# Attention into FFN on one core: transposes of four head pairs moved from TensorE to DMA, with the early slots rebuilt around them

## The chip, the cores and the metric

One core of one Trainium2 chip. The metric is device time in microseconds (us); lower is better. Verdicts compare fast runs of one kernel with fast runs of the kernel before, made on the same chip in the same rounds. PE is TensorE, DVE is VectorE, ACT is ScalarE, POOL is GpSimd, SP is SyncE. A DMA "lands" when all its data have arrived. An idle is "released" by the instruction or DMA whose end let the engine go on.

## The reference, cut to what matters

```python
# q, k, v: (8, 8, 576, 64) float32.  Sd = 144 (sequence pooled by 4)
out_d     = softmax(scale * mean4(q) @ mean4(k).T) @ mean4(v)      # pooled attention
out_local = softmax(where(|i - j| < 4, scale * q @ k.T, -1e9)) @ v # narrow band
x   = (repeat(out_d, 4) + out_local) as 4608 tokens x 512
out = (relu(x @ w_gate) * (x @ w_val)) @ w_out                     # d_ff = 1536
```

## The kernel before

Heads are handled two at a time, in 32 "pairs". Four pairs of heads make one batch entry, that is 576 tokens. The first four pairs are a fill phase. Then the program runs in "slots": slot s works on the attention of pair s + 4, and beside it on three of the twelve column tiles of the FFN of token chunk s // 4 (512 tokens). From slot 4 on each slot also computes one output tile y of the chunk before. PE, DVE, ACT, POOL and SP each execute their own instructions strictly in the order in which the code emits them.

q and k have to be transposed before the scores. Pairs 0 to 8 do it on PE, by 24 small matmuls into PSUM and copies back; these also give the pooled q and k. Pairs 9 on do it by one DMA transpose issued from SP, and DVE sums by four afterwards (`emit_pool`).

```python
NTP = 9                                   # pairs below this are transposed on PE

def emit_load(hp):                        # on the GpSimd queue, fp32 to fp16 (but for the first q)
    ...
    elif hp < NTP:                        # one DMA for q, one for k
    else:                                 # one DMA per head: two for q, two for k
    ...
def emit_qkT(hp):
    nc.sync.dma_start_transpose(out=qkT[hp % 4][...], in_=qk16[hp % NL]...)

def emit_slot(s, gate):
    c, jj, hp = s // 4, 3 * (s % 4), s + LEAD
    ...
    emit_in(hp + 4)                       # loads, four pairs ahead
    if NTP <= hp + 3 < NP:
        emit_qkT(hp + 3)                  # DMA transpose, three pairs ahead
    if s == 0:
        ...                               # ends with emit_qkT_pe(hp + 1, 2, 3)
    if s <= 5:
        ...
        emit_s2t(hp - 1, gate)            # values of the pair before; then on ACT: Ln, gate, Exp; on DVE: xn, xT
    ...
    if s == 4:
        emit_y(c - 1, s % 4, 1)           # first y tile: 12 matmuls
    else:
        emit_h(c, jj, 0)()                # FFN column tile: 8 matmuls, relu on ACT, product on DVE
    emit_s1(hp, 4)                        # scores of this pair, exponentials
    if s == 4:
        emit_h(c, jj, 0)()
    emit_h(c, jj + 1, 1)()
    if s == 4:
        emit_vd(hp, 5)
    else:
        emit_qkT_pe(hp + 1, 4, 0, True)   # transposes of the next pair on PE
    return emit_h(c, jj + 2, 3)
```

The weights arrive in slices on the same GpSimd queue: a quarter of w_gate and w_val with each of pairs 3, 5, 6 and 7, and all of w_out, in four pieces, after pair 8.

The softmax here doesn't subtract the row's maximum and nothing guards it: scores larger than these inputs give would overflow.

Of the kernel before, what the change touches and what calls it, by code (L numbers as in the profile page):

```python
# [57 lines left out]
def kernel(  # L58
# [22 lines left out]
    NCH = NTOK // TCH  # L81
    NJJ = D_FF // 128
    LEAD = 4
    NTP = 9
    NVP = 9
    NK = NJJ // 2
    B0 = 1
# [88 lines left out]
    def emit_load(hp):  # L176
        r = hp % NL
        b, off = head_off(hp)
        for src, dst in ((q, qk16[r][:, 0, :]), (k, qk16[r][:, 1, :])):
            if hp == 0 and src is q:  # L180
                nc.sync.dma_start(
                    q32.rearrange("p (n d) -> p n d", d=64),
                    _dap(src, off, [[D, 96], [NQ * D, 2 * NB], [1, D]]),
                )
                nc.scalar.copy(out=dst, in_=q32)
            elif hp < NTP:
                nc.gpsimd.dma_start(
                    dst.rearrange("p (n d) -> p n d", d=64),
                    _dap(src, off, [[D, 96], [NQ * D, 2 * NB], [1, D]]),
                )  # L190
            else:
                dv = dst.rearrange("p (j h d) -> p j h d", h=2, d=64)
                for hh in range(2):
                    nc.gpsimd.dma_start(  # L194
                        dv[:, :, hh, :],
                        _dap(src, off + hh * S * D, [[D, 96], [NQ * D, NB], [1, D]]),
                    )
        base = off - 3 * D
        t = vw[r][:, :, 0:64]
        n = 2 * NB  # L200
        if off == 0:
            nc.gpsimd.dma_start(
                t[:, 1:, :], _dap(v, base + NQ * D, [[D, WK], [NQ * D, n - 1], [1, D]])
            )
            nc.gpsimd.dma_start(t[3:WK, 0, :], _dap(v, 0, [[D, WK - 3], [1, D]]))
            nc.gpsimd.dma_start(t[0:3, 0, :], _dap(v, 0, [[D, 3], [1, D]]))
        elif b == B - 1 and hp % NPB == NPB - 1:
            nc.gpsimd.dma_start(
                t[:, 0 : n - 1, :], _dap(v, base, [[D, WK], [NQ * D, n - 1], [1, D]])
            )  # L210
            last = base + (n - 1) * NQ * D
            nc.gpsimd.dma_start(t[0:99, n - 1, :], _dap(v, last, [[D, 99], [1, D]]))
            nc.gpsimd.dma_start(t[99:WK, n - 1, :], _dap(v, last, [[D, WK - 99], [1, D]]))
        else:
            nc.gpsimd.dma_start(t, _dap(v, base, [[D, WK], [NQ * D, n], [1, D]]))  # L215
        if hp >= NVP:
            nc.gpsimd.dma_start(
                v4[hp % NV4], _dap(v, off, [[4 * D, 72], [72 * 4 * D, 4], [1, 4 * D]])
            )
# [13 lines left out]
                op=ALU.add,  # L233
            )

    def emit_qkT_pe(hp, b0, b1, b0_last=False):
        r, r4, r2 = hp % NL, hp % 4, hp % 2
        sv = qk16[r].rearrange("p i (h j d) -> p i h j d", h=2, d=64)
        blocks = list(range(2 * NB))
        if hp == 0:  # L240
            blocks = blocks[NB:] + blocks[:NB]
        elif b0_last:
            blocks = blocks[4:] + blocks[:4]
        for n in blocks:
            lo = 120 * (n % 4)
            bank = b0 if n < 4 else b1 + n // 4 - 1
# [10 lines left out]
        act, dve = nc.scalar.copy, nc.vector.tensor_copy  # L257
        if hp == 0:
            plan = ((2, 1, act), (2, 0, act), (1, 1, dve), (1, 0, dve), (0, 1, act), (0, 0, dve))
        elif b0_last:  # L260
            plan = ((1, 1, act), (1, 0, act), (2, 1, dve), (2, 0, dve), (0, 1, dve), (0, 0, act))
        else:
            plan = ((0, 1, act), (0, 0, act), (1, 1, dve), (2, 1, dve), (2, 0, dve), (1, 0, act))
        for i, pooled, copy in plan:
# [30 lines left out]
            out=vd[hp % 3].rearrange("p c (x d) -> p c x d", x=3)[:, :, 0:3:2, :], in_=o[0:72]  # L295
        )

    def emit_s1(hp, p0):
        r4, r2 = hp % 4, hp % 2
        for c in range(2):  # L300
            for hh in range(2):
                lo = 64 * hh
                nc.tensor.matmul(  # L303
                    out=ps[0:72, p0 + 2 * c + hh, 288:432],
                    lhsT=qkd[r2][lo : lo + 64, 1, bass.ts(c, 72)],
                    rhs=qkd[r2][lo : lo + 64, 0, :],
                    start=True,
                    stop=True,
                )
            for j in range(3 * c, 3 * c + 3):  # L310
                for hh in range(2):
                    lo = 64 * hh
                    k0 = S + NQ * j - 3
                    nc.tensor.matmul(  # L314
                        out=ps[:, p0 + 2 * c + hh, NQ * (j % 3) : NQ * (j % 3) + NQ],
                        lhsT=qkT[r4][lo : lo + 64, k0 : k0 + 128],
                        rhs=qkT[r4][lo : lo + 64, NQ * j : NQ * j + NQ],
                        start=True,
                        stop=True,
                    )  # L320
        for g in range(2):
            o = ee[r2][:, :, 288 * g : 288 * g + 288]
            nc.scalar.activation(  # L323
                out=o, in_=ps[0:WK, p0 + 2 * g : p0 + 2 * g + 2, 0:288], func=AF.Exp, scale=scale
            )
            nc.vector.tensor_tensor(  # L326
                out=o,
# [1 line left out]
                in1=_sap(masks_sb, (0, WK), 288 * g, [[0, 2], [1, 288]]),  # L329
                op=ALU.mult,  # L330
            )
        nc.scalar.activation(  # L332
            out=ed[r2][:, :, 0 : 2 * SD].rearrange("p h (c t) -> p c h t", c=2),
            in_=ps[0:72, p0 : p0 + 4, 288:432].rearrange("p (c h) t -> p c h t", c=2),
            func=AF.Exp,
            scale=scale / 16.0,
        )

    def emit_s2(hp, bank, pu):
        r2 = hp % 2  # L340
# [38 lines left out]
                op=ALU.mult,  # L379
            )  # L380

    def emit_s2t(hp, between):
        r2 = hp % 2
        e, d = ee[r2], ed[r2]
        for g in range(2):
            for hh in range(2):
                nc.tensor.matmul(
                    out=ps[64 * hh : 64 * hh + 64, 4 + g, 0:288],
                    lhsT=ones_sb[0:WK, 0:64],
                    rhs=e[:, hh, 288 * g : 288 * g + 288],  # L390
                    start=True,
                    stop=True,
                )
            for c in range(2):
                for hh in range(2):
                    nc.tensor.matmul(  # L396
                        out=ps[64 * hh : 64 * hh + 64, 4 + g, 288:360],
                        lhsT=ones_sb[0:72, 64:128],
                        rhs=d[:, hh, c * SD + 72 * g : c * SD + 72 * g + 72],
                        start=(c == 0),  # L400
# [2 lines left out]
        for g in range(2):  # L403
            for j in range(3):
                for hh in range(2):
                    nc.tensor.matmul(
                        out=ps[64 * hh : 64 * hh + 64, 2 + g, NQ * j : NQ * j + NQ],
                        lhsT=vw[hp % NL][:, NB * hh + 3 * g + j, 0:64],
                        rhs=e[:, hh, 288 * g + NQ * j : 288 * g + NQ * j + NQ],
                        start=True,  # L410
# [2 lines left out]
            for c in range(2):  # L413
                for hh in range(2):
                    nc.tensor.matmul(
                        out=ps[64 * hh : 64 * hh + 64, 2 + g, 288:360],
                        lhsT=vd[hp % 3][:, c, 128 * hh : 128 * hh + 64],
                        rhs=d[:, hh, c * SD + 72 * g : c * SD + 72 * g + 72],
                        start=(c == 0),
                        stop=(c == 1),  # L420
                    )
        r, x = rden[r2], xn[r2]
        nc.scalar.activation(out=r, in_=ps[:, 4:6, 0:360], func=AF.Ln)  # L423
        between()
        nc.scalar.activation(out=r, in_=r, func=AF.Exp, scale=-1.0)  # L425
        nc.vector.tensor_tensor(out=x, in0=ps[:, 2:4, 0:360], in1=r, op=ALU.mult)  # L426
        emit_xsum(hp)

    def emit_xsum(hp):
# [216 lines left out]
    def emit_wo(i):  # L646
# [2 lines left out]
            _dap(moe_w_out, 384 * i * D_MODEL, [[D_MODEL, 128], [128 * D_MODEL, 3], [1, D_MODEL]]),  # L649
        )  # L650

    after_load = {3: 0, 5: 1, 6: 2, 7: 3}

    def emit_in(hp):
# [5 lines left out]
        if hp in after_load:  # L660
            emit_wslice(after_load[hp])
        if hp == 8:
            for i in range(4):
                emit_wo(i)

    def emit_warm(n):
# [52 lines left out]
    def emit_slot(s, gate):  # L719
        c, jj, hp = s // 4, 3 * (s % 4), s + LEAD  # L720
        if NVP <= hp + 1 < NP:
            emit_vd_pool(hp + 1)
        emit_in(hp + 4)
        if NTP <= hp + 3 < NP:
            emit_qkT(hp + 3)
        if s == 0:
# [2 lines left out]
            emit_h_mm(c, jj, 3, 0, range(1))  # L729
            emit_x_pe(hp - 1, 0)  # L730
            emit_h(c, jj, 3, ((0, range(1, 4)), (1, range(3, 4))))()
            emit_s1(hp, 2)
            emit_h(c, jj + 1, 0)()
            emit_vd(hp, 6)
            emit_qkT_pe(hp + 1, 2, 3)
            return emit_h(c, jj + 2, 3)
        if s <= 5:
            if s == 5:
                emit_pool(hp)
            elif s < 4:  # L740
                emit_vd(hp, 1)
            emit_s2t(hp - 1, gate)
        elif gate:
            gate()
        if s > 4:
            if hp < NP:
                emit_y(c - 1, s % 4, 1 if s == 5 else 2, 6 if s == 5 else 2, lambda: emit_s1(hp, 4))
            else:
                emit_y(c - 1, s % 4, 2)
            if hp < NVP:  # L750
                emit_vd(hp, 3)
            if hp + 1 < NP:
                emit_pool(hp + 1)
            emit_h(c, jj, 0)()
            if 24 <= s < 28:
                emit_wt(s - 24)
            if hp < NP:
                emit_s2w(hp)
            emit_h(c, jj + 1, 1)()
            gate = emit_h(c, jj + 2, 0)  # L760
            if hp < NP:
                gate()
                emit_xsum(hp)
                return None
            return gate
        if s == 4:
            emit_y(c - 1, s % 4, 1)
        else:
            emit_h(c, jj, 0)()
        emit_s1(hp, 4)  # L770
        if s == 4:
            emit_h(c, jj, 0)()
        emit_h(c, jj + 1, 1)()
        if s == 4:
            emit_vd(hp, 5)
        else:
            emit_qkT_pe(hp + 1, 4, 0, True)
        return emit_h(c, jj + 2, 3)

    with tc.manual_schedule(engines={ET.PE, ET.DVE, ET.Activation, ET.SP, ET.Pool}):  # L780
        nc.scalar.dma_start(cst_sb[:, 960:1080], cst_dr[:, 960:1080])
# [57 lines left out]
```

## Time and profile before

| | before |
|---|---|
| median of 3 runs | 354.75 us (354.53 to 354.94) |
| span of the profiled run | 352.6 us |
| PE busy | 343.5 us (97%) |
| start on PE of slots 1 to 5 | 32.92, 41.22, 49.51, 57.46, 67.18 us |
| last load of pairs 5 to 8 landed | 26.2, 33.0, 40.0, 46.8 us |

The page of the kernel before cuts the span into 40 slices. A digit is a busy share in tenths; PEclk is the granted clock of TensorE in tenths; the DMA row is the mean busy share of the 16 DMA engines.

```profile
PE   6999999999999999999999999999999999999996
PEclk9999999999999999999999999999999999999999
DMA  9999999999999999999999999940000000101013
```

PE is full from the second slice on, at full clock. The DMA engines are full too, up to the 26th slice. In the first 57 us the reason is a backlog: loads wait in the GpSimd queue behind one another, and the view of DMA issues gives this for the last load of pair 8 (the last number is us from issue to landing; it was issued at 36.1 us):

```profile
qk<-in_k_dram POOLq DMA_DIRECT2D x1, 144.0 KB, 10.7
```

So it took 10.7 us to land at 46.8 us. The next view has one row for each of the slots 1 to 4: the stretch, its length, then busy time of each engine with the number of instructions, the granted clock, the DMA share and GB/s.

```profile
32.92:41.22 8.30, 8.04 (x106) 4.52 (x104) 5.09 (x10) 6.11 (x12) 5.32 (x8) 1.00 1.74 186
41.22:49.51 8.29, 8.03 (x105) 4.52 (x103) 5.09 (x10) 6.10 (x12) 4.42 (x6) 1.00 1.69 188
49.51:57.46 7.95, 7.69 (x98) 4.09 (x96) 5.09 (x10) 6.11 (x12) 3.78 (x5) 1.00 1.69 184
57.46:67.18 9.72, 9.72 (x91) 4.95 (x90) 6.60 (x8) 5.66 (x10) 9.55 (x13) 1.00 1.87 166
```

Slots 1 and 2 take 8.3 us, with 0.26 us of PE idle. PE's own timeline (start, length, what) shows what an ordinary slot pays for the transposes, and how slot 4 is ordered:

```profile
46.59 0.82 PE L248 MATMUL ps<-cst_sb,qk 96*64 96x120 f16 x24
...
58.36 2.76 PE L530 MATMUL ps<-wo_sb,gT 128*128 128x512 f16 x12
...
61.56 1.04 PE L505 MATMUL ps<-xT,wg_sb 128*128 128x512 f16 x4
```

The 24 transposing matmuls (L248) hold PE for 0.75 us to the next start (47.34 us). In slot 4, which starts at 57.46 us, the y tile (L530) runs from 58.36 to 61.05 us. Meanwhile DVE computes the attention output of pair 7:

```profile
60.06 0.91 DVE L426 TENSOR_TENSOR xn<-ps,rden 128x720 f16<-128x720 f32 x1
61.00 0.76 DVE L431 TENSOR_TENSOR xT<-xn 128x576 f16<-128x576 f16 x1
```

xT (L431) ends at 61.76 us, 4.3 us after the start of the slot. The FFN matmuls of chunk 1, which need it, start at 61.56 us, and the one that needs pair 7 is their fourth. It comes in time: PE has no idle in this slot. In all of 24 to 90 us PE's waits come to 1.1 us; three of them are for xn (the fourth, of 0.3 us, is for ee in slot 5):

```profile
PE ps L505 <- DVE xn L426: 0.8, 3, 0.3
```

### The profile page before, as it was taken

The numbers are of one execution on the slowest core, as the hardware profiler recorded it, in microseconds if no ns is written. First come the engines' busy times: TensorE is split into PE (matmuls) and PEld (weight loads), VectorE is DVE, ScalarE is ACT, GpSimd is POOL, SyncE is SP. The second block draws the span as 40 slices with busy tenths as digits, with TensorE's granted clock in tenths as the row PEclk, the third lists the DMA queues.
The fourth block names the chain that finished last, engine by engine and source line by source line (L and its number), as shares of the span: only waits on it lengthen the run. The fifth ranks groups of instructions, "written<-read, shape, count | busy, mean of one in ns | idle before, by whom it ended". The sixth has DMA issues, their size and how long they took to land.

```text
span 352.6 us, 7540 instructions
## 1 busy us (share of the span) xinstructions
PE 343.5 (97%) x2947; PEld 187.0 (53%) x2947; DVE 248.3 (70%) x397; ACT 214.0 (61%) x370; POOL 189.5 (54%) x233
## 2 busy tenths in 40 slices
PE   6999999999999999999999999999999999999996
PEld 3665555545545555555555544455555465655575
DVE  5894666687786677788887787776777655354581
ACT  3867776676677766666666667667667533333332
POOL 8986557999999877777778877722100000000000
PEclk9999999999999999999999999999999999999999
DMA  9999999999999999999999999940000000101013
GB/s 153 168 171 187 182 194 153 180 167 194 176 146 166 171 131 131 134 134 118 134 119 138 113 131 140 123 95 30 32 31 32 33 30 30 46 30 46 15 47 119
DMA packets 168770, 40.26 MB, mean 114 GB/s; under 512 B 150080, under 2 KB 165664, under 8 KB 168736
## 3 DMA queue, kind: packets, MB, share of 16 engines
q0 software_dynamic: 132960, 22.93, 86.1%
q1 hardware_dynamic: 32176, 10.55, 17.6%
q10 hardware_dynamic: 3600, 6.32, 5.3%
q8 instruction: 23, 0.38, 0.5%
q14 instruction: 11, 0.09, 0.1%
HBM read 46.45 MB, written 9.44 MB: 159 GB/s over the span
## 4 chain that ended last, share of the span: by engine, by line
PE 89%; DVE 4%; ACT 4%; DMA 1%; issue 1%; POOLq 0%
PE ps L505 50%; PE ps L530 18%; PE ps L592 8%; PE ps L448 3%; PE ps L248 2%; PE ps L314 2%; PE ps L303 2%; PE ps L456 2%; DMA qk<-in_k_dram 1%; DVE xn L426 1%; ACT rden L423 1%; DVE xo L375 1%; ACT rden L425 1%; DVE ee L326 1%; ACT r L520 1%
## 5 line engine op out<-in xcount | busy, mean ns | idle before, releaser
L505 PE MATMUL ps<-xT,wg_sb 128*128 128x512 f16 x432 | 111.5, 379 | 0.9 <-DVE xn L426 0.8
L505 PE MATMUL ps<-xT,wv_sb 128*128 128x512 f16 x432 | 111.2, 379 | 0.5 <-DVE gT L521 0.5
L521 DVE TENSOR_TENSOR gT<-r,ps 128x512 f16<-128x512 f16 x108 | 71.8, 683 | 49.2 <-PE ps L505 32.4
L520 ACT ACTIVATE r<-ps 128x512 f16<-128x512 f32 x108 | 64.0, 593 | 38.2 <-PE ps L505 35.7
L530 PE MATMUL ps<-wo_sb,gT 128*128 128x512 f16 x288 | 70.1, 380 | 0.0
L505 PEld LDWEIGHTS <-wv_sb 128*128 128x128 f16 x432 | 42.1, 98 | 51.4 <-issue 0.8
L472 DVE TENSOR_TENSOR xn<-ps,rden 64x720 f16<-64x720 f32 x46 | 41.6, 905 | 39.2 <-ACT rden L469 38.5
L505 PEld LDWEIGHTS <-wg_sb 128*128 128x128 f16 x432 | 39.7, 97 | 39.5 <-issue 0.7
L323 ACT ACTIVATE ee<-ps 112x576 f16<-112x576 f32 x64 | 38.1, 647 | 26.2 <-PE ps L314 25.4
L466 ACT ACTIVATE rden<-ps 64x720 f32<-64x720 f32 x46 | 35.2, 764 | 12.9 <-PE ps L456 12.3
L530 PEld LDWEIGHTS <-gT 128*128 128x128 f16 x288 | 26.1, 98 | 30.0
L326 DVE TENSOR_TENSOR ee<-ee,cst_sb 112x576 f16<-112x576 f16 x64 | 40.8, 674 | 1.3 <-ACT ee L323 1.1
L275 POOL TENSOR_TENSOR vd<-v 72x256 f16<-72x256 f32 x23 | 17.7, 770 | 44.2 <-PE ps L456 43.5
L194 POOL DMA_DIRECT2D qk<-in_q_dram x46 | 34.1, 744 | 4.2 <-DMA wo_sb<-in_moe_w_out_dram 2.8
L194 POOL DMA_DIRECT2D qk<-in_k_dram x46 | 33.2, 728 | 0.6 <-DMA qk<-in_k_dram 0.4
L215 POOL DMA_DIRECT2D vw<-in_v_dram x30 | 28.4, 946 | 4.9 <-PE ps L396 1.4
L229 DVE TENSOR_REDUCE qkd<-qkT 128x288 f16<-128x1152 f16 x23 | 30.8, 1341 | 0.0
L274 POOL TENSOR_TENSOR v<-v 72x512 f32<-72x512 f16 x23 | 30.5, 1327 | 0.3
L538 ACT COPY y_sb<-ps 128x512 f32<-128x512 f32 x24 | 14.1, 587 | 17.2 <-PE ps L530 17.2
L431 DVE TENSOR_TENSOR xT<-xn 128x576 f16<-128x576 f16 x28 | 22.3, 798 | 0.2
L448 PE MATMUL ps<-ee,vw 112*128 112x96 f16 x276 | 20.4, 205 | 0.3 <-DVE ee L326 0.3
L332 ACT ACTIVATE ed<-ps 72x576 f16<-72x576 f32 x32 | 20.5, 642 | 0.0
(97 smaller groups left out, 374.4 us busy)
## 6 DMA issues: line engine op xcount, KB each, us to landing
out_dram<-y_sb ACTq DMA_DIRECT2D x24, 256.0 KB, 4.0
vw<-in_v_dram POOLq DMA_DIRECT2D x30, 168.0 KB, 6.3
qk<-in_q_dram POOLq DMA_DIRECT2D x46, 72.0 KB, 3.4
qk<-in_k_dram POOLq DMA_DIRECT2D x46, 72.0 KB, 3.6
v<-in_v_dram POOLq DMA_DIRECT2D x23, 144.0 KB, 6.2
out_dram<-y_sb SPq DMA_DIRECT2D x22, 128.0 KB, 1.7
wg_sb<-in_moe_w_gate_dram POOLq DMA_DIRECT2D x4, 384.0 KB, 9.8
wv_sb<-in_moe_w_val_dram POOLq DMA_DIRECT2D x4, 384.0 KB, 10.7
```

What stands on the lines that cost most here:

```text
L194: nc.gpsimd.dma_start(dv[:, :, hh, :], _dap(src, off + hh * S * D, [[D, 96], [NQ * D, NB], [1, D]]),)
L229: nc.vector.tensor_reduce(out=qkd[hp % 2].rearrange("p i t -> p (i t)"), in_=qkT[hp % 4][:, 0 : 2 * S].rearrange("p (t f) -> p t f", f=4), ...
L274: nc.gpsimd.tensor_tensor(out=m, in0=t[:, :, 0:128], in1=t[:, :, 128:256], op=ALU.add)
L323: nc.scalar.activation(out=o, in_=ps[0:WK, p0 + 2 * g : p0 + 2 * g + 2, 0:288], func=AF.Exp, scale=scale)
L326: nc.vector.tensor_tensor(out=o, in0=o, in1=_sap(masks_sb, (0, WK), 288 * g, [[0, 2], [1, 288]]), op=ALU.mult,)
L448: nc.tensor.matmul(out=ps[:, bank, NQ * j : NQ * j + NQ], lhsT=vflat[:, v0 : v0 + 128], rhs=e[:, hh, lo : lo + NQ], start=True, stop=True,)
L466: nc.scalar.activation(out=r[lo : lo + 64], in_=ps[de : de + 64, 4 + 2 * hh : 6 + 2 * hh, 0:360], func=AF.Ln)
L472: nc.vector.tensor_tensor(out=x[lo : lo + 64], in0=ps[lo : lo + 64, 4 + 2 * hh : 6 + 2 * hh, 0:360], in1=r[lo : lo + 64], op=ALU.mult,)
L505: nc.tensor.matmul(out=pair(pp)[:, which, :], lhsT=w[:, kk, bass.ts(jj, 128)], rhs=xT[:, kk, c * TCH : (c + 1) * TCH], start=(kk == 0), st ...
L520: nc.scalar.activation(out=r1, in_=h1, func=AF.Relu)
L521: nc.vector.tensor_tensor(out=gT[c % 2][:, jj, :], in0=r1, in1=h2, op=ALU.mult)
L530: nc.tensor.matmul(out=y_ps, lhsT=gT[c % 2][:, jj, bass.ts(ty, 128)], rhs=wo_sb[:, jj, :], start=(jj == 0), stop=(jj == NJJ - 1),)
```

## The change

The intent is to take the transposing matmuls of pairs 5 to 8 off PE. The pairs go by DMA transposes, with DVE's sum by four in place of the pooled copies. Their q and k are then loaded by one DMA per head, two per tensor. The slots are rewritten: PSUM bank pairs rotate from slot to slot, the pooled exponential of a pair comes first, the first y tile moves from the start to the end of slot 4, and half of w_out is loaded after the q and k of pair 9.

```diff
-    NTP = 9
+    NTP = 5
@@ emit_load: between the loads of q, k and those of v
+        if hp == 9:
+            emit_wo(2)
+            emit_wo(3)
@@ emit_in
         if hp == 8:
-            for i in range(4):
+            for i in range(2):
                 emit_wo(i)
@@ emit_s1(hp, p0, p1=None, ed_first=False): scores may lie in two bank pairs that are not neighbours
+        base = (p0, p0 + 2 if p1 is None else p1)
+        def pooled():
+            nc.scalar.activation(
+                out=ed[r2]...,
+                in_=_sap(ps, (0, 72), 512 * base[0] + 288,
+                         [[512 * (base[1] - base[0]), 2], [512, 2], [1, 144]]),
+                func=AF.Exp, scale=scale / 16.0)
@@ slots; EARLY[s] is (numerator, denominator, first FFN tile, scores, scores), as bank pairs
+    EARLY = {1: (1, 2, 0, 2, 3), 2: (2, 3, 1, 0, 3), 3: (3, 0, 2, 0, 1), 4: (0, 1, 3, 1, 2)}
+        if s == 0:
+            emit_qkT(hp + 1)
+            emit_qkT(hp + 2)
         if NTP <= hp + 3 < NP:
             emit_qkT(hp + 3)
+        if s < 5:
+            num, den, h0, s0, s1 = EARLY[s]
+            gate()
+            emit_pool(hp)
+            emit_s2t(hp - 1, 2 * num, 2 * den)
+            emit_h(c, jj, h0)()
+            emit_s1(hp, 2 * s0, 2 * s1, True)
+            emit_h(c, jj + 1, num)()
+            emit_vd(hp, 2 * s0)
+            gate = emit_h(c, jj + 2, h0)
+            if s == 4:
+                emit_y(c - 1, 0, 0)
+            return gate
@@ (cut: the branches that these lines replace; slot 0 loses emit_qkT_pe(hp + 1))
```

More of the change, by code (lines that the diff above doesn't have):

```diff
@@ L234, in emit_pool, with emit_qkT_pe @@
             )
-    def emit_qkT_pe(hp, b0, b1, b0_last=False):
+    def emit_qkT_pe(hp, b0, b1):
         r, r4, r2 = hp % NL, hp % 4, hp % 2
@@ L241, in emit_qkT_pe @@
             blocks = blocks[NB:] + blocks[:NB]
-        elif b0_last:
-            blocks = blocks[4:] + blocks[:4]
         for n in blocks:
@@ L259, in emit_qkT_pe @@
             plan = ((2, 1, act), (2, 0, act), (1, 1, dve), (1, 0, dve), (0, 1, act), (0, 0, dve))
-        elif b0_last:
-            plan = ((1, 1, act), (1, 0, act), (2, 1, dve), (2, 0, dve), (0, 1, dve), (0, 0, act))
         else:
@@ L296, in emit_vd, with emit_s1 @@
         )
-    def emit_s1(hp, p0):
+    def emit_s1(hp, p0, p1=None, ed_first=False):
         r4, r2 = hp % 4, hp % 2
+        base = (p0, p0 + 2 if p1 is None else p1)
         for c in range(2):
@@ L303, in emit_s1 @@
                 nc.tensor.matmul(
-                    out=ps[0:72, p0 + 2 * c + hh, 288:432],
+                    out=ps[0:72, base[c] + hh, 288:432],
                     lhsT=qkd[r2][lo : lo + 64, 1, bass.ts(c, 72)],
@@ L314, in emit_s1 @@
                     nc.tensor.matmul(
-                        out=ps[:, p0 + 2 * c + hh, NQ * (j % 3) : NQ * (j % 3) + NQ],
+                        out=ps[:, base[c] + hh, NQ * (j % 3) : NQ * (j % 3) + NQ],
                         lhsT=qkT[r4][lo : lo + 64, k0 : k0 + 128],
@@ L320, in emit_s1 @@
                     )
+        def pooled():
+            nc.scalar.activation(
+                out=ed[r2][:, :, 0 : 2 * SD].rearrange("p h (c t) -> p c h t", c=2),
+                in_=_sap(
+                    ps,
+                    (0, 72),
+                    512 * base[0] + 288,
+                    [[512 * (base[1] - base[0]), 2], [512, 2], [1, 144]],
+                ),
+                func=AF.Exp,
+                scale=scale / 16.0,
+            )
+        if ed_first:
+            pooled()
         for g in range(2):
@@ L323, in emit_s1 @@
             nc.scalar.activation(
-                out=o, in_=ps[0:WK, p0 + 2 * g : p0 + 2 * g + 2, 0:288], func=AF.Exp, scale=scale
+                out=o, in_=ps[0:WK, base[g] : base[g] + 2, 0:288], func=AF.Exp, scale=scale
             )
@@ L331, in emit_s1 @@
             )
-        nc.scalar.activation(
-            out=ed[r2][:, :, 0 : 2 * SD].rearrange("p h (c t) -> p c h t", c=2),
-            in_=ps[0:72, p0 : p0 + 4, 288:432].rearrange("p (c h) t -> p c h t", c=2),
-            func=AF.Exp,
-            scale=scale / 16.0,
-        )
+        if not ed_first:
+            pooled()
     def emit_s2(hp, bank, pu):
@@ L380, in emit_s2, with emit_s2t @@
             )
-    def emit_s2t(hp, between):
+    def emit_s2t(hp, num, den, between=None):
         r2 = hp % 2
@@ L387, in emit_s2t @@
                 nc.tensor.matmul(
-                    out=ps[64 * hh : 64 * hh + 64, 4 + g, 0:288],
+                    out=ps[64 * hh : 64 * hh + 64, den + g, 0:288],
                     lhsT=ones_sb[0:WK, 0:64],
@@ L396, in emit_s2t @@
                     nc.tensor.matmul(
-                        out=ps[64 * hh : 64 * hh + 64, 4 + g, 288:360],
+                        out=ps[64 * hh : 64 * hh + 64, den + g, 288:360],
                         lhsT=ones_sb[0:72, 64:128],
@@ L406, in emit_s2t @@
                     nc.tensor.matmul(
-                        out=ps[64 * hh : 64 * hh + 64, 2 + g, NQ * j : NQ * j + NQ],
+                        out=ps[64 * hh : 64 * hh + 64, num + g, NQ * j : NQ * j + NQ],
                         lhsT=vw[hp % NL][:, NB * hh + 3 * g + j, 0:64],
@@ L415, in emit_s2t @@
                     nc.tensor.matmul(
-                        out=ps[64 * hh : 64 * hh + 64, 2 + g, 288:360],
+                        out=ps[64 * hh : 64 * hh + 64, num + g, 288:360],
                         lhsT=vd[hp % 3][:, c, 128 * hh : 128 * hh + 64],
@@ L422, in emit_s2t @@
         r, x = rden[r2], xn[r2]
-        nc.scalar.activation(out=r, in_=ps[:, 4:6, 0:360], func=AF.Ln)
-        between()
+        nc.scalar.activation(out=r, in_=ps[:, den : den + 2, 0:360], func=AF.Ln)
+        if between:
+            between()
         nc.scalar.activation(out=r, in_=r, func=AF.Exp, scale=-1.0)
-        nc.vector.tensor_tensor(out=x, in0=ps[:, 2:4, 0:360], in1=r, op=ALU.mult)
+        nc.vector.tensor_tensor(out=x, in0=ps[:, num : num + 2, 0:360], in1=r, op=ALU.mult)
         emit_xsum(hp)
@@ L731, in emit_slot @@
             emit_h(c, jj, 3, ((0, range(1, 4)), (1, range(3, 4))))()
-            emit_s1(hp, 2)
+            emit_s1(hp, 2, 4, True)
             emit_h(c, jj + 1, 0)()
-            emit_vd(hp, 6)
-            emit_qkT_pe(hp + 1, 2, 3)
+            emit_vd(hp, 2)
             return emit_h(c, jj + 2, 3)
-        if s <= 5:
-            if s == 5:
-                emit_pool(hp)
-            elif s < 4:
-                emit_vd(hp, 1)
-            emit_s2t(hp - 1, gate)
+        if s < 5:
[11 more added lines that the diff above has]
+            return gate
@@ L743, in emit_slot @@
+        if s == 5:
+            emit_pool(hp)
+            emit_s2t(hp - 1, 2, 4, gate)
         elif gate:
             gate()
-        if s > 4:
-            if hp < NP:
-                emit_y(c - 1, s % 4, 1 if s == 5 else 2, 6 if s == 5 else 2, lambda: emit_s1(hp, 4))
-            else:
-                emit_y(c - 1, s % 4, 2)
-            if hp < NVP:
-                emit_vd(hp, 3)
-            if hp + 1 < NP:
-                emit_pool(hp + 1)
-            emit_h(c, jj, 0)()
-            if 24 <= s < 28:
-                emit_wt(s - 24)
-            if hp < NP:
-                emit_s2w(hp)
-            emit_h(c, jj + 1, 1)()
-            gate = emit_h(c, jj + 2, 0)
-            if hp < NP:
-                gate()
-                emit_xsum(hp)
-                return None
-            return gate
@@ L766, in emit_slot @@
-        if s == 4:
-            emit_y(c - 1, s % 4, 1)
-        else:
-            emit_h(c, jj, 0)()
-        emit_s1(hp, 4)
-        if s == 4:
-            emit_h(c, jj, 0)()
-        emit_h(c, jj + 1, 1)()
-        if s == 4:
-            emit_vd(hp, 5)
-        else:
-            emit_qkT_pe(hp + 1, 4, 0, True)
-        return emit_h(c, jj + 2, 3)
+        emit_y(c - 1, s % 4, 1 if s == 5 else 2, 6 if s == 5 else 2, lambda: emit_s1(hp, 4))
+        if hp + 1 < NP:
+            emit_pool(hp + 1)
@@ L780 @@
+        emit_h(c, jj, 0)()
+        if 24 <= s < 28:
+            emit_wt(s - 24)
+        emit_s2w(hp)
+        emit_h(c, jj + 1, 1)()
+        emit_h(c, jj + 2, 0)()
+        emit_xsum(hp)
+        return None
     with tc.manual_schedule(engines={ET.PE, ET.DVE, ET.Activation, ET.SP, ET.Pool}):
```

## The prediction

> **What bounds it now.** The page has PE busy 343.5 of 352.6 us at granted clock 1.0, and the chain of waits is 89% PE. From 78 us on the chain holds nothing but PE until about 276 us, so whatever slots 0 to 5 gain or lose passes on one for one. Early on a second resource is full: until about 57 us the GpSimd queue streams loads without a break (windows view: 176 to 188 GB/s from 16 to 57 us, DMA share 1.7 to 2.0), and Pool waits for landings before it can issue. Loads of q/k take 8 to 11 us from issue to landing there. The last k of pairs 5, 6, 7, 8 lands at about 26.2, 33.0, 40.0, 46.9 us. Slots 1 to 5 start on PE at 32.9, 41.2, 49.5, 57.5 and 67.2 us (timeline).
>
> **Removed.** 24 transposing matmuls for each of pairs 5 to 8: 0.75 us of PE each in the chain, with about 0.1 us of switching, so 3.4 us, all on PE's path. Also their PSUM copies (about 1 us on DVE, 1.2 us on ACT per pair), which bound nothing. The 0.28 us that PE waits for xn (L426) in slots 1 to 3 stays: the pooling reduce (1.34 us) now stands before xn on DVE, about as long as what rotation frees.
>
> **Added.** Four DMA transposes (issue to landing 5.6 to 9.4 us, median 6.4; about 3 us of packets each), inside the full stretch. The Trainium skill ("DMA: Bandwidth & Descriptors", "Issuing engines are not separate DMA queues") says DMAs of all issuers share the same 16 engines; the trace agrees: with 717 transpose packets in one microsecond the load queue moved 41, where it moves about 1200 alone. So each transpose delays later loads by an estimated 1.2 to 2 us. Estimated landings of T5 to T8: 33, 41, 49, 57.5 us. DVE wants them at about 33.2, 40.7, 48.2, 55.5, so pairs 6 to 8 are 0.3 to 2 us late, accumulating to about 2 us, and DVE's order (reduce before xn, xT, gate products) hands this to PE.
>
> **Moved.** The y tile leaves the start of slot 4. There it covered (58.4 to 61.1 us) the chain Ln, Exp, xn, xT of pair 7, which ends 4.3 us after the slot's start; the first FFN matmul of chunk 1 with kk = 3 needs that xT, since chunk 1 holds tokens of batch 1. Now only s2t and three matmuls (1.55 us) precede it: PE stalls about 2.8 us in slot 4, and longer by however late T8 is. Split w_out loads let pair 9 land earlier; with y at about 65 us or later I expect no wait for w_out.
>
> **Sum.** -3.4 (transposes) +2.8 (slot 4) +2 (late transposes) = about +1.3 us: 356.0 us, range 353.6 to 359.5. Faster by over 2%: 0.01; within 2%: 0.96; slower by over 2%: 0.03. If every transpose landed in time, the sum would be about -0.6 us.
>
> **What would show it.** Right: slot 1 starts near 32.1; slot 4 has a PE idle of 2.5 us or more in front of an FFN matmul, released by DVE's xT (L444); DVE waits for transposes before L232 in slots 2 to 4; slot 5 starts at 67 to 70 us; slots 6 on keep 9.16 us. Wrong: no PE idle in slot 4; slots 1 to 3 at about 7.4 us each; slot 5 starting before 66 us.
>
> **What would make it wrong.** Transposes getting full service beside the backlog (then 354); transposes starved by the weight packets (then over 359); a PE idle of 4 us or more in slot 4 lowering the granted clock afterwards; w_out landing after y wants it.

## The result, and the profile after

| | before | after |
|---|---|---|
| median | 354.85 us (4 runs) | 365.06 us (363.31 to 366.8, 4 runs) |
| ratio of fast runs | | 1.0288 (1.0238 to 1.0339) |
| span of the profiled run | 352.6 us | 364.8 us |
| start on PE of slots 1 to 5 | 32.92, 41.22, 49.51, 57.46, 67.18 us | 32.40, 43.92, 54.82, 61.95, 78.71 us |
| last load of pairs 5 to 8 landed | 26.2, 33.0, 40.0, 46.8 us | 26.1, 36.3, 44.8, 53.6 us |
| DMA transposes of pairs 5 to 8 landed | | 36.2, 44.2, 52.9, 65.2 us |

A ratio is the mean time of one kernel's fast runs over that of the other's of the same rounds, so it is not quite the ratio of the medians. The profiled run of the changed kernel was its slowest, 366.8 us.

The same rows of the page show where it happened:

```profile
PE   6998879599999999999999999999999999999996
PEclk9999889699999999999999999999999999999999
```

Slices 4 to 9 hold the slots 1 to 4. PE has holes in slices 4, 5, 6 and 8, and the granted clock falls in slices 5, 6 and 8. From slice 9 on these two rows do not differ from before. The rows of the slots 1 to 4:

```profile
32.40:43.92 11.52, 8.92 (x79) 4.47 (x78) 5.64 (x8) 5.22 (x9) 7.29 (x10) 0.85 1.86 172
43.92:54.82 10.90, 8.86 (x80) 4.23 (x79) 5.82 (x8) 5.34 (x9) 7.02 (x10) 0.84 1.66 183
54.82:61.95 7.13, 7.13 (x81) 3.77 (x80) 5.82 (x8) 5.19 (x9) 4.07 (x6) 1.00 1.71 153
61.95:78.71 16.76, 12.17 (x92) 5.65 (x91) 7.17 (x9) 4.85 (x8) 10.10 (x13) 0.80 1.97 157
```

Slot 3 is what the change wanted: 7.13 us instead of 7.95. Slots 1, 2 and 4 take 3.2, 2.6 and 7.0 us more than before, and all three ran at a mean clock of 0.80 to 0.85. PE's waits, in total and by releaser, name three new stalls (smaller ones left out):

```profile
PE ps L518 <- DVE xT L444: 4.6, 1, 4.6
PE ps L303 <- DVE qkd L232: 2.4, 1, 2.4
PE ps L518 <- ACT ed L323: 2.0, 1, 2.0
```

PE's timeline places them: the idle before a row is in brackets, with what ended it.

```profile
34.17 1.03 PE L518 MATMUL ps<-xT,wv_sb 128*128 128x512 f16 x4
37.56 0.25 PE L303 MATMUL ps<-qkd 64*72 64x144 f16 x2 [2.36 <-DVE qkd L232]
...
49.27 1.86 PE L518 MATMUL ps<-xT,wg_sb 128*128 128x512 f16 x4 [2.04 <-ACT ed L323]
...
62.84 0.82 PE L518 MATMUL ps<-xT,wg_sb 128*128 128x512 f16 x3
68.25 0.59 PE L518 MATMUL ps<-xT,wg_sb 128*128 128x512 f16 x1 [4.59 <-DVE xT L444]
68.63 1.91 PE L518 MATMUL ps<-xT,wv_sb 128*128 128x512 f16 x4
```

The stall of 2.36 us in slot 1 is for the sum by four (L232) of a transpose that landed at 36.2 us. The stall of 2.04 us in slot 2 is released by ACT. The stall of 4.59 us in slot 4 is in front of the fourth FFN matmul and is released by xT. The row at 68.63 us also shows the clock: four matmuls take 1.91 us there, and 1.03 us at 34.17.

What xT waited for is on DVE:

```profile
65.24 1.35 DVE L232 TENSOR_REDUCE qkd<-qkT 128x288 f16<-128x1152 f16 x1 [2.43 <-DMA qkT<-qk]
66.51 0.90 DVE L439 TENSOR_TENSOR xn<-ps,rden 128x720 f16<-128x720 f32 x1
67.44 0.76 DVE L444 TENSOR_TENSOR xT<-xn 128x576 f16<-128x576 f16 x1
```

and the DMA transpose of pair 8 itself, issued at 53.81 us, has this entry:

```profile
L225 SPq DMA_TRANSPOSE qkT<-qk x1: 1472/1472/1472, 53.8 to 53.8; - x1
...
  DVE qkd L232: 2.4, 1
...
DMA to landing us min/median/max: 11.4/11.4/11.4
```

It landed 11.4 us after its issue, at 65.2 us. The reduce, xn and xT follow within 3.0 us, PE resumes at 68.25, and the rest of slot 4, to 78.71, takes 10.46 us.

### The profile page after: what moved, and what is told of

The parts are those of the page before. It is cut to its first block, busy times and chain, and to the rows that moved or that the text cites. A ratio compares the mean times of both kernels' runs of the same rounds, so it can differ in the third digit from the quotient of the medians.

```text
span 364.8 us, 7357 instructions
## 1 busy us (share of the span) xinstructions
PE 346.5 (95%) x2851; PEld 185.9 (51%) x2851; DVE 249.8 (68%) x389; ACT 210.7 (58%) x358; POOL 194.4 (53%) x241
## 4 chain that ended last, share of the span: by engine, by line
PE 83%; DMA 7%; DVE 4%; ACT 3%; issue 2%; ACTq 0%; POOLq 0%
PE ps L518 47%; PE ps L543 17%; PE ps L605 7%; DMA qkT<-qk 6%; PE ps L461 3%; PE ps L314 2%; PE ps L303 2%; PE ps L469 2%; DMA qk<-in_k_dram 2%; DVE xn L439 1%; PE ps L249 1%; DVE xo L387 1%; DVE xT L444 1%; DVE gT L534 1%; ACT rden L435 0%
## 5 line engine op out<-in xcount | busy, mean ns | idle before, releaser
L518 PE MATMUL ps<-xT,wg_sb 128*128 128x512 f16 x432 | 114.1, 385 | 7.0 <-DVE xT L444 4.6
L518 PE MATMUL ps<-xT,wv_sb 128*128 128x512 f16 x432 | 113.9, 386 | 0.5 <-DVE gT L534 0.5
L518 PEld LDWEIGHTS <-wg_sb 128*128 128x128 f16 x432 | 40.1, 98 | 41.4 <-issue 3.8
L194 POOL DMA_DIRECT2D qk<-in_q_dram x54 | 40.1, 747 | 10.4 <-PE ps L518 4.0
L194 POOL DMA_DIRECT2D qk<-in_k_dram x54 | 39.2, 731 | 7.5 <-DMA qk<-in_k_dram 4.4
L543 PEld LDWEIGHTS <-gT 128*128 128x128 f16 x288 | 26.2, 98 | 30.2
L342 DVE TENSOR_TENSOR ee<-ee,cst_sb 112x576 f16<-112x576 f16 x64 | 38.3, 631 | 3.7 <-ACT ee L339 3.3
L232 DVE TENSOR_REDUCE qkd<-qkT 128x288 f16<-128x1152 f16 x27 | 36.3, 1343 | 5.3 <-DMA qkT<-qk 5.3
L273 POOL TENSOR_TENSOR v<-v 72x512 f32<-72x512 f16 x23 | 30.1, 1309 | 0.3
L551 ACT COPY y_sb<-ps 128x512 f32<-128x512 f32 x24 | 14.1, 587 | 20.3 <-PE ps L543 20.3
L444 DVE TENSOR_TENSOR xT<-xn 128x576 f16<-128x576 f16 x28 | 24.0, 857 | 0.2
```

Source lines behind the costliest of these rows:

```text
L194: nc.gpsimd.dma_start(dv[:, :, hh, :], _dap(src, off + hh * S * D, [[D, 96], [NQ * D, NB], [1, D]]),)
L232: nc.vector.tensor_reduce(out=qkd[hp % 2].rearrange("p i t -> p (i t)"), in_=qkT[hp % 4][:, 0 : 2 * S].rearrange("p (t f) -> p t f", f=4), ...
L273: nc.gpsimd.tensor_tensor(out=m, in0=t[:, :, 0:128], in1=t[:, :, 128:256], op=ALU.add)
L342: nc.vector.tensor_tensor(out=o, in0=o, in1=_sap(masks_sb, (0, WK), 288 * g, [[0, 2], [1, 288]]), op=ALU.mult,)
L518: nc.tensor.matmul(out=pair(pp)[:, which, :], lhsT=w[:, kk, bass.ts(jj, 128)], rhs=xT[:, kk, c * TCH : (c + 1) * TCH], start=(kk == 0), st ...
L543: nc.tensor.matmul(out=y_ps, lhsT=gT[c % 2][:, jj, bass.ts(ty, 128)], rhs=wo_sb[:, jj, :], start=(jj == 0), stop=(jj == NJJ - 1),)
```

## The experiments

Two theories stood at the start. Theory A: the stalls add up, so each that is removed pays its length. Theory B: the transpose of pair 8 alone decides when slot 4 resumes; earlier stalls only fill the time in which PE would wait for it anyway. A third question was what the half clock costs.

### e1_split: the pooled exponential of slot 2 in two parts

```diff
+            if base[1] - base[0] > 2:
+                for c in range(2):
+                    nc.scalar.activation(
+                        out=ed[r2][:, :, c * SD : (c + 1) * SD],
+                        in_=ps[0:72, base[c] : base[c] + 2, 288:432],
+                        func=AF.Exp, scale=scale / 16.0)
+                return
```

> The changed kernel with one edit: in slot 2, where the scores lie in bank pairs 0 and 3, the pooled exponential is issued as two activations (one per pair) instead of one whose access pattern strides over the pairs between. Theory A (every stall adds to the time): the 2.04 us stall in slot 2, released there by that activation, goes, with about 1.7 us of half clock behind it, so about 361.4 us. Theory B (only the landing of the transpose of pair 8 sets where slot 4 resumes, so earlier stalls are absorbed by it): the stall in slot 2 goes, but the first FFN matmul with kk = 3 in slot 4 still runs at about 68 us and the time stays within 1 us of the changed kernel, 364 to 366 us, with a longer idle in slot 4 instead. If the stall in slot 2 stays, it was not the access pattern.

Measured: 364.6 us, ratio to before 1.0267 (1.0209 to 1.0325), so no different from the changed kernel. PE's timeline of this kernel, after the scores of slot 2 and in slot 4:

```profile
45.57 1.21 PE L527 MATMUL ps<-xT,wg_sb 128*128 128x512 f16 x4 [0.24 <-DVE xn L448]
...
69.97 0.59 PE L527 MATMUL ps<-xT,wg_sb 128*128 128x512 f16 x1 [8.47 <-DVE xT L453]
```

The wait for ACT in slot 2 is gone; in the trace's record of this matmul, too, the semaphore it waits for changed from ACT's to DVE's. So it was the access pattern: one activation that reads bank pairs 0 and 3 by a stride was ordered against pair 2, which lies between them. And removing it paid nothing that these runs show: the stall in slot 4 grew from 4.59 to 8.47 us. The transpose of pair 8 landed at 66.9 us here, 1.7 us later than in the changed kernel although slot 2 was faster. This is theory B.

### e2_warm4 and e12_warm4 with e11_after: work in the idle of slot 4

```diff
+            if s == 4:
+                emit_h_mm(c, jj, h0, 0, range(3))
+                emit_warm(20, 4)          # 20 matmuls on zeros
+                emit_h(c, jj, h0, ((0, range(3, 4)), (1, range(4))))()
+            else:
+                emit_h(c, jj, h0)()
```

> The changed kernel with 20 matmuls on zeros (4.3 us of PE) between the third and the fourth FFN matmul of slot 4, where PE idled 4.59 us; nothing else is changed, and the fourth matmul can't start earlier than before. If part of the loss is the half clock from 66.3 to 73.2 us, caused by the idle: the granted clock stays 1.0 there, the rest of slot 4 takes 8.0 us instead of 10.5, and the time falls by about 2.4 us, to about 362.6. If the half clock has another cause or costs nothing: no change, 365 us. If PE work were the bound, 4.3 us would be added.

Measured: 364.11 us against 365.06 for the changed kernel, in other rounds. PE's timeline in slot 4:

```profile
62.25 0.82 PE L518 MATMUL ps<-xT,wg_sb 128*128 128x512 f16 x3
62.91 4.48 PE L682 MATMUL ps<-zero_sb 128*128 128x512 f16 x20
67.81 0.38 PE L518 MATMUL ps<-xT,wg_sb 128*128 128x512 f16 x1 [0.42 <-DVE xT L444]
```

Here 20 more matmuls cost nothing, PE resumes at 67.81, and from there every matmul runs at full speed: the rest of slot 4 takes 8.16 us (to 75.97) instead of 10.46. The gain in time was below the 2.4 us expected, so both kernels were run again in the same rounds.

> The changed kernel itself once more, for a comparison on the same chip in the same rounds with the next run. 363 to 366 us.

> The kernel with 20 zero matmuls in the idle of slot 4 once more, in the same rounds as the changed kernel. If half clock in slot 4 is part of the loss: faster than the changed kernel by 1.5 to 2.5 us. If the difference seen in the first comparison of the medians (0.95 us) was chance: within 0.7 us of it.

Measured: 364.92 us for the changed kernel and 363.86 with the zero matmuls; the means differ by 0.9 us, which lies between the two outcomes expected and is not clear of the scatter (the intervals of the ratios to before, 1.0215 to 1.0279 and 1.0204 to 1.0254, overlap). In these two traces the part of slot 4 after the resumption took 9.45 us (67.04 to 76.49) without the zero matmuls and 8.16 us (66.36 to 74.52) with them. So the idle brings the half clock of slot 4, and it costs 1.3 to 2.3 us there in the traces; a gain in time is not shown. One reason can be seen: the test is not free. In the trace of e12_warm4 the transpose of pair 8 landed at 62.2 us and xT was done at 65.14, but the zero matmuls held PE until 66.36.

### e3_light: fewer weight loads beside the transposes

```diff
-    after_load = {3: 0, 5: 1, 6: 2, 7: 3}
+    after_load = {3: 0}
-                lhsT=w[:, kk, bass.ts(jj, 128)],
+                lhsT=w[:, kk, bass.ts(jj % 3, 128)],
@@ one piece of w_out with pair 8, the others in slots 5, 7 and 9
-                rhs=wo_sb[:, jj, :],
+                rhs=wo_sb[:, jj % 3, :],
```

> The changed kernel with less load traffic (result wrong on purpose): slices 1 to 3 of w_gate and w_val are never loaded (the matmuls read slice 0 again), and only the first piece of w_out is loaded early, the others in slots 5, 7 and 9. PE work is the same. If the late transposes come from sharing the DMA engines with the weight stream: transposes of pairs 5 to 8 land within 7.5 us of their issue and before the reduce wants them, no idle before the scores of slot 1, and what is left is the slot 2 stall (2 us) and the slot 4 stall that the order alone gives (2.6 us): 355.5 to 359.5 us. If DMA transposes are slow by themselves: 8 to 11 us from issue to landing as now, and 363 us or more.

Its output is wrong, which doesn't matter for the time. Measured: 358.2 us (355.34 to 358.84), ratio 1.0062 (1.001 to 1.0114). The transposes landed at 33.2, 36.3, 41.7 and 47.4 us, 6.3 to 8.6 us after their issue, and DVE waited for none of them. Two idles are left on PE in slots 1 to 4, one of 2.04 us in slot 2, released by ACT (ed), and this one:

```profile
61.22 0.40 PE L515 MATMUL ps<-xT,wg_sb 128*128 128x512 f16 x1 [3.15 <-DVE xT L441]
```

The first is the stall of slot 2 again, 2.04 us to the hundredth. The second is in slot 4 although the transpose had landed at 47.4 us: it is the price of the order alone, 3.15 us here. One window of half clock (61.45 to 64.86 us) followed it.

### e4_yearly: the first y tile back at the start of slot 4

```diff
             emit_s2t(hp - 1, 2 * num, 2 * den)
+            if s == 4:
+                emit_y(c - 1, 0, 4)
             emit_h(c, jj, h0)()
@@
-            if s == 4:
-                emit_y(c - 1, 0, 0)
@@ and all four pieces of w_out after pair 8 again
```

> The changed kernel with the first y tile back at the start of slot 4 (between s2t and the FFN matmuls, PSUM bank 4) and all four w_out loads back with pair 8. If the late landing of the transpose of pair 8 is the bound: the fourth FFN matmul of slot 4 still waits for xT until about 68 us, y fills 2.6 us of that wait, the half clock is shorter, and the time is about 360 us (358.5 to 362). If the moved y tile is the whole cause of the loss in slot 4: its stall goes wholly, about 356 us. If the w_out loads delay the transpose of pair 8 further: 362 us or more.

Measured: 362.43 us (361.09 to 364.36), ratio 1.0201 (1.0147 to 1.0255). This is just above the 358.5 to 362 us expected. The transpose of pair 8 landed at 65.6 us and the fourth matmul ran at 68.62, as theory B says; y filled part of the wait and left 1.72 us. Moving y back gains 2.2 us against e1_split of the same rounds (2.6 against the first runs of the changed kernel) and doesn't rescue the kernel.

### e5_ideal: all suspected causes taken away at once

The edits of e3_light, e1_split and e4_yearly's y together, with only the first piece of w_out early.

> The light-load kernel (result wrong on purpose: slices 1 to 3 of w_gate and w_val not loaded, three of four w_out pieces loaded late), with both other suspected stalls taken away: the pooled exponential of slot 2 split in two, and y back at the start of slot 4. If the loss of the changed kernel consists of late transposes, the slot 2 stall, the slot 4 stall and the half clock that follows idle, and of nothing else, no idle over 0.4 us is left in slots 1 to 4, the clock stays 1.0, and the 3.4 us of PE transposes come out as a gain: about 351.5 us (350.5 to 352.5). If something else in the rebuilt slots costs time: 353 us or more.

Measured: 351.23 us (350.95 to 352.18), ratio 0.9883 (0.9855 to 0.991). Its output is wrong, which doesn't matter for the time. The rows of slots 1 and 4 (2 and 3 take 7.13 and 7.12 us, all of it busy, at full clock):

```profile
32.56:39.69 7.13, 7.13 (x80) 3.77 (x80) 5.81 (x8) 5.19 (x9) 6.98 (x10) 1.00 2.06 163
53.94:63.66 9.72, 9.72 (x91) 4.95 (x91) 6.77 (x9) 5.29 (x9) 8.12 (x11) 1.00 1.85 175
```

No idle, full clock. So under this light load nothing else in the rebuilt slots costs time, and all gains together are worth 4.0 us by the medians (355.22 before in these rounds). The 3.4 us predicted for the transposes fit: the waits of 0.26 us for xn in slots 1 to 3, which the prediction kept, went too (0.78 us in all), and account for the rest.

### e6_rot: the rebuilt order without DMA transposes

```diff
-    NTP = 5
+    NTP = 9
@@ slot 0 and slots 1 to 3; no emit_pool before slot 5
-            emit_vd(hp, 2 * s0)
+            if s < 4:
+                emit_vd(hp, 2 * s1 + 1)
+                emit_qkT_pe(hp + 1, 2 * s1, 2 * s0)
+            else:
+                emit_vd(hp, 2 * s0)
```

> The changed kernel without its DMA transposes: pairs 5 to 8 are transposed on PE as before, while the rotating bank pairs, the first y tile at the end of slot 4 and the split w_out loads stay. If the rebuilt order costs by itself: the slot 2 stall (about 2 us, by the pooled exponential over pairs 0 and 3) and a slot 4 stall of about 2.7 us, released by xT, are there without any late transpose, perhaps with one window of half clock: 358.5 to 362 us. If the transposes by DMA are the whole loss: 355 us.

Measured: 360.18 us (359.03 to 360.67), ratio 1.0125 (1.0096 to 1.0154), as expected. PE's idles in slots 2 and 4:

```profile
46.71 1.02 PE L518 MATMUL ps<-xT,wg_sb 128*128 128x512 f16 x4 [2.04 <-ACT ed L323]
...
63.57 0.38 PE L518 MATMUL ps<-xT,wg_sb 128*128 128x512 f16 x1 [2.29 <-DVE xT L444]
```

The order alone brings both stalls, 4.3 us together, with no DMA transpose before pair 9. In the profiled run the clock stayed full.

### e7_tonly: the DMA transposes alone, in the order of before

```diff
-    NTP = 9
+    NTP = 5
@@ slot 0: emit_qkT(hp + 1) and emit_qkT(hp + 2), no emit_qkT_pe; slots 1 to 3: no emit_qkT_pe
-            if s == 5:
+            if hp >= NTP:
                 emit_pool(hp)
-            elif s < 4:
+            if s < 4:
                 emit_vd(hp, 1)
```

> The kernel before with the DMA transposes of pairs 5 to 8 alone: its own slot order, banks, y at the start of slot 4, w_out loads with pair 8. If the landing of the transpose of pair 8 (about 65 us) is the bound, it comes out like the changed kernel with y moved back: 360 to 363 us, with slot 5 starting at 73 to 75 us. If the DMA transposes alone are harmless, 351.5 to 353 us; if the rotation of banks is what makes waiting for them dear, clearly below 360.

Measured: 363.88 us (361.97 to 364.8), ratio 1.0227 (1.019 to 1.0263); slot 5 started at 77.1 us in the profiled run, later than expected. DVE's row in slot 4:

```profile
65.91 1.35 DVE L229 TENSOR_REDUCE qkd<-qkT 128x288 f16<-128x1152 f16 x1 [5.79 <-DMA qkT<-qk]
```

DVE stood 5.79 us for the transpose of pair 8, and everything behind the reduce in DVE's order stood with it. PE met this wait at the last matmul of y, which needs a gate product (gT) that stands behind the reduce; xT was no stall here:

```profile
67.91 0.61 PE L530 MATMUL ps<-wo_sb,gT 128*128 128x512 f16 x1 [3.01 <-DVE gT L521]
```

So the transposes alone lose nearly as much as the whole change (8.7 us by the medians), and the order alone loses 5 us; together they lose 10. They don't add. The traces suggest why: both hold up PE in slot 4, and it can go on only when the later of the two is done.

### e9_wolate: no w_out beside the transpose of pair 8

```diff
-        if hp == 9:
-            emit_wo(2)
-            emit_wo(3)
-        if hp == 8:
-            for i in range(2):
+        if hp == 9:
+            for i in range(4):
                 emit_wo(i)
```

> The changed kernel with all four w_out loads behind the loads of pair 9, so that none of them is in the queue while the transpose of pair 8 runs. If the 1 KB packets of w_out are what stretches that transpose from 8 to 11.4 us: it takes about 8 us, lands at 62 us or earlier, the fourth FFN matmul of slot 4 runs at about 65, and the time falls by 3 to 4 us to 361 to 362 us, unless y (at about 73 us) then has to wait for w_out. If the transpose is slow for the general backlog: 11 us as before, and 364 us or more.

Measured: 362.69 us (362.12 to 363.1), ratio 1.0197 (1.0173 to 1.0221). The transpose of pair 8, issued at 53.85 us:

```profile
DMA to landing us min/median/max: 6.5/6.5/6.5
```

So it was the w_out stream that stretched it: 6.5 us instead of 11.4. (While its packets moved, 102 packets of 1 KB from w_out moved too, and 462 in the changed kernel.) The transpose of pair 9, which now met all of w_out, took 14.1 us. PE's idle in slot 4 fell to the share of the order:

```profile
65.71 0.38 PE L515 MATMUL ps<-xT,wg_sb 128*128 128x512 f16 x1 [2.28 <-DVE xT L441]
```

The time fell by 2.2 us against e11_after of the same rounds, less than the 3 to 4 us expected. The trace shows the reason: the transpose landed at 60.3 us, before slot 4 began (61.71 us), so the stalls of slots 1 and 2 (6.4 us of idle, with a window of half clock) were no longer hidden behind it.

### e13_halves: the loads cut in two

```diff
+            elif 5 <= hp < NTP:           # before, with one DMA per head
+                for hh in range(2):
+                    nc.gpsimd.dma_start(dst...[:, NB * hh : NB * hh + NB, :], ...)
```

> The kernel before with only one edit: q and k of pairs 5 to 8 are loaded in two DMAs per tensor (one per head) instead of one, as the DMA transposes need them; transposes stay on PE. If it is the transposes' share of the DMA engines that delays the loads in the changed kernel: the last loads of pairs 5 to 8 land at 26, 33, 40 and 47 us, within 1 us of the kernel before. If it is the larger number of DMA issues: they drift towards the 26, 36, 45 and 54 us of the changed kernel.

Measured (one look): 354.48 us. The last loads landed at 25.8, 32.8, 39.7 and 46.8 us. For pair 8 (the median of its last two loads, issued at 39.3 and 40.1 us):

```profile
qk<-in_k_dram POOLq DMA_DIRECT2D x2, 72.0 KB, 6.7
```

The same kind of load in the changed kernel, issued at 44.7 us:

```profile
qk<-in_k_dram POOLq DMA_DIRECT2D x1, 72.0 KB, 8.9
```

The number of issues delays nothing. It is the transposes: the last loads of pairs 6, 7 and 8 come 3.3, 4.8 and 6.8 us later behind one, two and three of them, 2.3 us for each on average. e7_tonly, with the order of before, has the transpose of pair 8 landing at 65.9 us, so the new order is not the cause.

### e8_t8, e14_t8 and e10_t78: can the stretch bear one or two?

e8_t8 is before with `NTP = 8`. e14_t8 adds room in slot 4: the reduce of pair 8 after xT of pair 7 on DVE, and the scores after the first FFN tile. e10_t78 is e14_t8 with `NTP = 7`.

> The kernel before with only pair 8 transposed by DMA. Its last load lands at 46.9 us and the scores of pair 8 come after y in slot 4, at about 60 us, so a transpose of 11 us (58 us) is just in time and the 0.84 us of PE transposes are saved: 354.0 to 354.6 us. If the transpose takes over 12 us beside the four w_out loads, its lateness eats the gain: 355 us or more.

> The kernel before with pair 8 alone transposed by DMA and with the same room for lateness as in the run with pairs 7 and 8. If one transpose in this stretch is borne: 354.2 to 354.7 us, 0.8 us below the kernel before, with all runs at a clock of 0.998 or more. If the load queue has no room even for one: same as before or slower, with some runs at a lower clock.

> The kernel before with pairs 7 and 8 transposed by DMA, where the loads land longest before their use, and with room for lateness: in slot 4 the reduce of pair 8 comes after xT of pair 7 on DVE, and the scores of pair 8 come after the first FFN tile. If lateness and order are all that is wrong with the DMA transposes: 1.7 us of PE work saved and no stall, about 353.5 us (352.9 to 354.2). If the two transposes delay loads that others need (w_out for y at 57 us, pair 9): 355 us or more.

| | median | ratio to before |
|---|---|---|
| e8_t8 | 355.43 us | 0.9996 (0.9969 to 1.0022) |
| e14_t8 | 354.64 us | 0.9987 (0.9963 to 1.0011) |
| e10_t78 | 357.95 us | 1.0013 (0.9969 to 1.0058) |

None is shown to beat before. The median of e14_t8 lies in the range expected, but the interval of its ratio includes 1, and three of its six runs had a clock below 0.998. In the trace of e8_t8 the transpose took 11.3 us and the run, its fastest, 353.63 us; the other five were slower, and the record does not show why. The six runs of e10_t78 fall into two groups: two took 354.2 and 354.4 us at a clock of 0.999 or more, four took 357.8 to 360.5 at 0.988 to 0.994; two of these four the ratio leaves out. The only trace is of a fast run, so the cause is not shown; that the margin with two transposes is so small that most runs fall into idle and half clock is a guess. No kernel with a right result is shown to be better than before.

## Why the prediction was wrong

The prediction was 356.0 us, 353.6 to 359.5; measured was 365.06. Point by point:

- **What bounds it, and that gains and losses in slots 0 to 5 pass on: right.** After slot 5 the slots keep their 9.16 us (scores of pairs 11 and 12 at 99.55 and 108.71 us).
- **3.4 us of PE work saved: right.** e5_ideal measures 4.0 us, with the three waits of 0.26 us for xn that the prediction kept.
- **The stall from moving y, 2.8 us in slot 4: right.** It is 2.29 us in e6_rot and 3.15 in e3_light, where no transpose is late.
- **The late transposes, +2 us: this is the term that failed.** The mechanism was named, and the sizes were wrong. The prediction had DVE wanting the transpose of pair 8 at 55.5 us and the landing at 57.5 us; it landed at 65.2, so the lateness was 9.7 us in place of 2. Two parts make the 7.7 us. First, each transpose delays later loads by 2.3 us on average, not 1.2 to 2: the last load of pair 8 came at 53.6 us, where the middle of my range gives 46.9 + 3 x 1.6 = 51.7. Second, the transpose then took 11.4 us, not the 6 or so assumed, because the w_out packets were in the queue (e9_wolate: 6.5 us with most of them gone). The prediction had named this case (transposes starved by the weight packets, over 359 us) but left it out of the sum. I had taken the median of all transposes of the trace (6.4 us), about half of which ran after 128 us, where the DMA engines moved 130 GB/s (128 to 230 us), and applied it to a stretch of 176 to 188.
- **Half clock: named as a risk, given no weight.** From the landing of pair 8 to slot 5 the traces give 11.2 us at full clock: 3.0 for the reduce, xn and xT, and 8.16 for the rest of slot 4. From 57.5 us this leads to 68.7, inside the predicted 67 to 70. 57.5 + 7.7 + 11.2 is 76.4, and slot 5 started at 78.7. The missing 2.3 us are the half clock after the idle (10.46 us in place of 8.16, e2_warm4).
- **The stall in slot 2: not foreseen.** 2.04 us with one cause, the strided activation over bank pairs 0 and 3. In the changed kernel no cost of it is seen, as it is hidden behind pair 8 (e1_split); in e6_rot nothing hides it.
- **DVE waiting for transposes in slots 2 to 4: half right.** The waits were in slots 1 and 4 (2.9 and 2.4 us). In slots 2 and 3 the slots themselves had become late, so nothing waited.
- **"Slot 5 starts at 67 to 70 us": wrong,** 78.7, for the reasons above. **No wait for w_out: right.**

That the late landing of pair 8 is the bound, and not the sum of stalls, is shown by e1_split and e4_yearly. That the lateness comes from sharing the DMA engines is shown by e3_light, e9_wolate and e13_halves. Not settled: why the first packets of a transpose start about 4 us after its issue in the backlogged stretch (30.1 for 26.2 us, 57.9 for 53.8), but 2.1 us after it in e9_wolate for pair 8 and 1.5 us in e3_light for pair 5.

Which idle brings half clock can be read from the traces. In each trace the clock changes only at points that lie 3.41 us or a multiple of it apart, so each trace has a grid of intervals. What counts is how much PE idles inside one interval. Here are two neighbouring intervals of the changed kernel and then two of e6_rot (the stretch, its length, PE busy; the third number from the right is the granted clock):

```profile
45.86:49.27 3.41, 1.37 (x21) 0.72 (x20) 2.46 (x4) 1.47 (x4) 2.06 (x3) 1.00 1.71 182
49.27:52.69 3.42, 3.42 (x9) 1.19 (x9) 0.92 (x2) 1.61 (x3) 1.84 (x3) 0.50 1.90 164
...
59.39:62.81 3.42, 1.89 (x37) 1.14 (x36) 1.65 (x3) 1.59 (x3) 1.45 (x2) 1.00 2.37 144
62.81:66.22 3.41, 2.65 (x26) 1.31 (x26) 1.39 (x2) 1.46 (x3) 2.92 (x4) 1.00 1.84 143
```

The stall of 2.04 us of slot 2 lies wholly in one interval, and the next one is at half clock. In e6_rot the grid cuts the stall of 2.29 us in two, 1.5 and 0.75 us, and the clock stays full. Counted over all 16 traces (intervals that began at full clock; the ends of matmuls are modelled), half clock followed all 11 intervals with 2.04 us of idle or more, none with 1.54 us or less, and 5 of the 8 between.

On what the skill says: the sharing of the 16 engines, cited in the prediction, holds here (2.3 us of delay to the loads for each transpose). The Trainium skill, "DMA: Bandwidth & Descriptors", "Queues, rings and completion order", says each engine takes turns between queues packet by packet. That fits e9_wolate: a transpose of 256-byte packets took 11.4 us beside 462 packets of 1 KB and 6.5 us beside 102; the turns themselves were not measured. "TensorE: Matmul & The Clock Gate", "What's actually happening", gives half rate after an idle window of about 3.4 us and says that this window runs freely. The traces agree with the length (one, two or three times 3.41 us at half clock) and with the free running: two traces of the same kernel, e2_warm4 and e12_warm4, have points of the grid at 36.2 and at 34.9 us. They do not agree that a whole window must be idle (2.04 us was enough).

## What to carry to other kernels

Work moved from a full engine to DMA must be costed with the queue as it is in that stretch, not with the median landing time of the whole trace; and its first victim is every later load in the same stretch. Find the one arrival that all later work waits for, and compute the gain from there: earlier savings and earlier stalls are both absorbed by it. When a long filler is moved in an in-order queue, look up what finished under its cover, and count idle of about 2 us or more on PE with the half clock that may follow it.

## What the Trainium skill lacked or had wrong

- "Advanced Engine Details and Errata", "X-Bar Transpose (TRN2)", calls transpose DMAs as fast as regular ones. Here each transpose of 288 KB delayed the loads behind it by 2.3 us on average. The loads of a pair with a slice of both weights (288 + 168 + 768 KB, as the view of DMA issues counts) came every 6.9 us, so 288 KB of loads take 1.6 us by an estimate from that rate. From issue to landing the transposes of pairs 5 to 8 took 6.3 to 12.8 us over all runs; no page gives a latency beside a full queue.
- "DMA: Bandwidth & Descriptors", "Latency and other measured facts", gives about 0.6 us to the first byte for DMAs issued from SP. In the backlogged stretch the first packets of the transposes came 3.9 to 4.1 us after issue, in e3_light 1.5 to 4.2 us.
- "TensorE: Matmul & The Clock Gate", "HAM oscillation", warns of idle gaps over about 3.4 us. Shorter ones are enough: in the changed kernel half clock came after idles of 2.36 and 2.04 us as well; in e6_rot idles of 2.04 and 2.29 us did not bring it in the profiled run, where the grid cut both in two.
- No page says that a matmul may be made to wait for an activation whose access pattern strides over the matmul's PSUM banks without reading them (2.04 us in slot 2).
